# Where the retention of a two-layer network is computed: token tiles of 512, 384, 512, 512 and 384, each prepared during the tile before it

## The chip, the core and the metric

The kernel runs on one core of a Trainium2 chip. The metric is the device time of one execution in microseconds; lower is better. The engines are named as the profile names them: PE (TensorE matmuls; PEld are its weight loads), DVE (VectorE), ACT (ScalarE), POOL (GpSimd) and SP (SyncE, here the engine that issues every DMA).

## The reference, cut to what matters

```python
scores = scale * np.matmul(q, k.transpose(0, 1, 3, 2))      # 4 x 8 heads, 576 tokens, 64 dims
ret = scores * Dmat                                         # gamma ** (i - j), 0 above the diagonal
x = np.matmul(ret, v)        # "retention"; then [2304 tokens, 512]
h = x @ w_in                 # 512 x 2048
g = np.maximum(h, 0.0) + np.log1p(np.exp(-np.abs(h)))       # softplus
x = g @ w_out                # 2048 x 512
r = np.maximum(x @ w2_in, 0.0)
out = (r * r) @ w2_out
```

The weights are float64 in memory and everything else is float32.

## The kernel before

**Two phases of matrix products.** The 2304 tokens are cut into tiles. In the first phase (softplus) the five tiles have 512, 448, 448, 448 and 448 tokens, in the second (squared relu) 384, 512, 512, 512 and 384. Each tile takes 16 steps, one for each 128 of the 2048 hidden features. Step j does on PE the first product of step j (`g1`, L336, out `ph`) and the second product of step j - 2 (`g2`, L405, out `acc`). A float32 product is made of three passes, so each is 12 matmuls; in the first phase each of the 24 matmuls of a step streams as many columns as the tile has tokens. Between the two products lie, for step j, three ACT functions (L350 to L352), three DVE operations (`softplus_b`, L357 to L363), a cast on ACT (L383) and a subtraction on DVE (L384) that make the two parts `gh` and `gl`.

**Weights.** Each of the 32 blocks of weights of a phase comes as float64 (512 KB) through one of three stages and is turned into a high and a low float32 part (`split_w`): two ACT operations (L121, L122), DVE L126 and L130, ACT L138, DVE L139. In the first tile `pump` does about two blocks in each step; the blocks of the second phase follow in the last tile of the first phase and the first tile of the second.

**Retention.** It runs in 36 chunks of 64 tokens, nine for each sequence. `step_s` (scores and state) does 8 heads x 2 matmuls (L237, L243), a masking on DVE (L247) and a copy of the state on ACT (L249). `step_o` (output) does 8 matmuls (L259) and a multiplication on DVE (L275). `scale_v` weighs the values of a later chunk on DVE (L222). The four buffers of chunks are loaded by SP (L208, L212, 256 KB each). Chunks 0 to 7, the first tile, come ahead of everything; this part is not touched.

**Where the other 28 chunks go.** `attend` spreads them, in halves (`tick_first`: scores; `tick_second`: output), over the first XEND = 29 steps, so over the first tile and most of the second: one half is recorded behind the ACT functions of a step, the other behind `softplus_b`. The result of tile 1 stays on chip (`x_raw[1]`). The results of tiles 2 to 4 are written, in place of the chunk's keys, to the DRAM arrays `x1d` (L285) and loaded a tile ahead by `load_x` (L428) into the one buffer `xr`. At the end of a tile `split_x` (L316 to L319) turns `xr` into the operands `xh` and `xl` of the next tile.

**What sets the order.** Ahead of the steps the order is written by hand. In the steps a scheduler arranges the recorded instructions on each engine; each engine then runs its own list in that order.

Of the kernel before, what the change touches and what calls it, by code (L numbers as in the profile page):

```python
# [16 lines left out]
P = 128  # L17
D = 64
CN = 64  # tokens of a chunk of the retention
SCN = 9  # chunks of a sequence  # L20
LOADS = 4  # chunks on chip
STAGES = 3  # weights on chip as they come
XEND = 29  # steps of the first product that carry the retention
# Tiles of tokens of the two phases: start, length.
TILES = ((0, 512), (512, 448), (960, 448), (1408, 448), (1856, 448))
TILES2 = ((0, 384), (384, 512), (896, 512), (1408, 512), (1920, 384))
# Columns of the constants' array: 1 - 2^-23, 0.49, weights of v, the causal mask (the latter two in the
# lower half of the partitions), and weights of the output.
# [6 lines left out]
def kernel(  # L35
# [12 lines left out]
    """Products of float32 matrices as three passes: each operand is the exact sum of two parts  # L48
    that float32r holds, hi (rounded) and lo (the rest), and hi*hi, hi*lo and lo*hi are summed in
    PSUM; lo*lo lies below float32's last bit.  # L50

    Retention runs in chunks of 64 tokens, with every head in the free dimension. Two operands are
    stacked in the partitions: [q, transposed; masked scores] against [state; v] gives a chunk's
    output. With i counted from the sequence's start, v takes gamma^-i, and the output scale *
    gamma^i; the state, the sum of k * v over the chunks before, then grows in PSUM without decay.
    """
# [32 lines left out]
    x1d = [dram.tile([P, n // CN, KD, CN], F32, name=f"x1d{t}") for t, (_, n) in enumerate(TILES)]  # L89
    x2d = dram.tile([KD, P, NT], F32, name="x2d")  # L90

    # ---------------------------------------------------------------- weights
# [15 lines left out]
    def split_w(phase, kind, f):  # L108
        """The two words of each float64 to float32 hi and lo, in steps.

        2^-112 times the upper word, read as a float32, has float32's exponent in place of
        float64's (values below float32's range go to 0). Shifted by 3 bits, with the sign put back
        and with 3 bits for the lower word, it is the float32. The lower word's upper half is
        mapped to 0 to 7, which keeps the mean error at 0.
        """
# [45 lines left out]
    def pump_step():  # L161
        """A step of the next weights' split; loads others into the stage that a whole one frees."""
        if not splitting:
            m = n_split[0]
            if m == len(items):
                return
            pump_load(m + 1)
            splitting.append(split_w(items[m][0], items[m][2], items[m][3]))
            n_split[0] += 1
        if next(splitting[0]):  # L170
            splitting.clear()
            pump_load(n_split[0] + STAGES)

    def pump(count):
        """Splits the next weights."""
        for _ in range(count):
            while True:
                pump_step()
                if not splitting:
                    break  # L180

    # -------------------------------------------------------------- retention
# [45 lines left out]
    def step_s(c, split):  # L228
        """Scores of chunk c, with keys in the partitions, and the state after it."""
# [6 lines left out]
        for h in range(H):  # L236
# [4 lines left out]
            if go_on:  # L241
                # One start clears what the whole bank held.
                nc.tensor.matmul(  # L243
                    st[LO, h, :], lhsT=kk[HI, h, :], rhs=sv[HI, h, :],
                    start=c % SCH == 0 and h == 0, stop=True, skip_group_check=True,
                )
# [4 lines left out]
    def step_o(c, ps):  # L251
# [16 lines left out]
        elif t == 1:  # L268
# [3 lines left out]
        else:  # L272
            # In place of the chunk's keys, which nothing reads any more.
            x = qkv[:, 1, 0:KD, :]
        nc.vector.tensor_tensor(out=x, in0=po, in1=xw, op=ALU.mult)  # L275
        if t == 0:
            # Nothing reads the operands of a product yet.
# [6 lines left out]
        if t > 1:  # L284
            nc.sync.dma_start(out=x1d[t][:, m], in_=x)  # L285
# [3 lines left out]
    def tick_first(split=False):  # L289
        """Scores and state of chunk k."""  # L290
        c = tick[0]
        if c < NCH:
            step_s(c, split)

    def tick_second(ps_o, load=True):
        """Output of chunk k - 1; loads run ahead."""
# [7 lines left out]
    # ------------------------------------------------------------------ GEMMs  # L304
    def split_x(raw, phase, n):
        """raw -> a tile's operands of the first product."""
# [34 lines left out]
    def softplus_a(key, n):  # L341
        """e = exp(-|h|), ln(1 + e), and a bound of log1p(e) from below that is sharp for small e.

        1 + e is rounded, which spoils the logarithm of small e: it is taken a last bit lower, and
        e - e^2/2 takes over where that is more.
        """
# [76 lines left out]
    def load_x(phase, t0, n):  # L423
        raw = xs.tile([P, 512 * KD], F32, tag="xr", name="xr")
        if phase == 0:
            t, _ = tile_of(t0)
            raw = raw.rearrange("p (m a b) -> p m a b", a=KD, b=CN)
            nc.sync.dma_start(out=raw[:, :n // CN], in_=x1d[t])  # L428
        else:
            raw = raw.rearrange("p (a b) -> p a b", a=KD)  # L430
            nc.sync.dma_start(
                out=raw[:, :, :n], in_=x2d[:, :, t0:t0 + n].rearrange("k p n -> p k n")
            )
        return raw

    # --------------------------------------------------------------- schedule
# [3 lines left out]
    # Chunks that have to be through before each tile of the first phase.  # L440
# [9 lines left out]
    def keep_warm(count):  # L450
        """Products that nothing reads: TensorE's clock stays up while the operands come."""
# [36 lines left out]
    half = [0]  # L488
    rest = 2 * (NCH - need[0])

    def attend(j, h2):
        """Attention's half ticks, spread evenly over the first steps."""
        pos = 2 * j + h2 + 1
        want = min(rest, -(-rest * pos // (2 * XEND)))
        while half[0] < want:
            if half[0] % 2 == 0:
                tick_first()
            else:
                tick_second(ps_at)
                scale_v(tick[0] - 2 + LOADS)  # L500
            half[0] += 1

    def weights(j):
        """How many weights of the first phase are split by step j."""
# [10 lines left out]
    for j, (b, f) in enumerate(steps):  # L515
# [11 lines left out]
        attend(j, 0)  # L527
        if j >= 1:
            split_g(j - 1, blocks[steps[j - 1][0]][2])
        if ph == 0:  # L530
            pump(max(0, weights(j) - n_split[0]))
        if j >= 2:
# [5 lines left out]
        attend(j, 1)  # L538
# [8 lines left out]
        if f == KF - 1 and b + 1 < len(blocks):  # L547
            split_x(x_next[0] if b else x_raw.pop(1), blocks[b + 1][0], blocks[b + 1][2])
            if b + 2 < len(blocks):
                x_next[0] = load_x(*blocks[b + 2])  # L550
# [11 lines left out]
def _by_dims(a):  # L562
    """[B, H, S, D] -> chunk, dimension, head, token of the chunk."""
# [7 lines left out]
def _by_tokens(a):  # L571
    """[B, H, S, D] -> chunk, token of the chunk, head, dimension."""
# [7 lines left out]
def _constants(n_heads, head_dim):  # L580
    """Decay weights and the causal mask: they depend on shapes alone."""
# [48 lines left out]
```

## Time and profile before

| | |
|---|---|
| runs of the kernel before | 912.48, 913.0, 913.43 us; median 913.0 |
| span of the profiled execution, first to last instruction | 913.3 us |
| own time of the profiled execution | not listed apart; its span lies within the runs above |
| PE busy | 896.1 us (98%), 5478 matmuls |
| DVE busy | 517.6 us (57%) |
| ACT busy | 429.3 us (47%) |
| granted TensorE clock, mean | 0.992 of full speed |
| DMA | 74.20 MB, mean 81 GB/s |

Busy time is the union of the records of an engine. A matmul's record is longer than its distance to the next one, since matmuls are pipelined; the length of a run of matmuls is therefore read from start to start. The first operands of a product exist at 39 us, the second tile's products begin at about 170 us, and the second phase begins at 507 us. Stretches below are given in us from the start of the span.

### The profile page before, as it was taken

How to read it: one execution, taken by the hardware profiler on the slowest of the kernel's cores; microseconds unless marked ns; L12 is line 12 of the kernel's file. 1: busy time of each engine (PE TensorE's matmuls, PEld its weight loads, DVE VectorE, ACT ScalarE, POOL GpSimd, SP SyncE). 2: the span in 40 equal slices, each digit the busy share in tenths (PEclk: the TensorE clock that was granted, in tenths of full speed). 3: DMA queues.
4: the chain of work that ended last, by engine and by line, in shares of the span. 5: the costliest groups of instructions: out<-in, count | busy, mean ns of one | idle time of the engine just before them, and what ended most of it. 6: DMA issues, size and time to landing. Idle time of an engine off the chain costs nothing.

```text
span 913.3 us, 13514 instructions
## 1 busy us (share of the span) xinstructions
PE 896.1 (98%) x5478; PEld 765.7 (84%) x5478; DVE 517.6 (57%) x849; ACT 429.3 (47%) x751; POOL 12.3 (1%) x16
## 2 busy tenths in 40 slices
PE   7999999999999999999999999999999999999998
PEld 6876777788899999999999998888888888888997
DVE  2799999966555547456985799522332233223322
ACT  2588777643454455444875598322222222222222
POOL 2300000000000000000000000000000000000000
PEclk8899999999999999999999999999999999999999
DMA  9867577743111002001520465200020001000100
GB/s 247 202 168 234 163 217 206 216 119 88 42 47 41 0 1 81 1 1 36 179 93 0 156 206 164 81 1 0 1 93 1 1 22 59 1 1 1 46 1 35
DMA packets 39181, 74.20 MB, mean 81 GB/s; under 512 B 3280, under 2 KB 25552, under 8 KB 38992
## 3 DMA queue, kind: packets, MB, share of 16 engines
q1 hardware_dynamic: 39120, 73.35, 26.7%
q8 instruction: 43, 0.70, 0.3%
q14 instruction: 18, 0.15, 0.1%
HBM read 61.15 MB, written 12.19 MB: 80 GB/s over the span
## 4 chain that ended last, share of the span: by engine, by line
PE 77%; DVE 10%; DMA 8%; ACT 3%; issue 2%; SPq 0%; POOL 0%; POOLq 0%; ACTq 0%; DVEq 0%
PE acc L405 37%; PE ph L336 36%; DMA wi_raw<-in_moe_w_in_dram 4%; DVE ct L130 2%; DMA wo_raw<-in_moe_w_out_dram 2%; DMA ch<-in_kv_dram 1%; PE po L259 1%; PE st L237 1%; DVE wo_raw L126 1%; DVE wol L139 1%; DVE wil L139 1%; DVE gl L384 1%; PE cold L453 1%; DVE wi_raw L126 1%; DVE l L360 1%
## 5 line engine op out<-in xcount | busy, mean ns | idle before, releaser
L336 PE MATMUL ph<-xh,wih 128*128 128x512 f32 (+2 forms) x640 | 240.3, 376 | 1.3 <-ACT xh L279 0.4
L336 PE MATMUL ph<-xh,wil 128*128 128x512 f32 (+2 forms) x640 | 238.0, 372 | 0.3 <-DVE wil L139 0.3
L336 PE MATMUL ph<-xl,wih 128*128 128x512 f32 (+2 forms) x640 | 159.0, 370 | 0.0
L336 PEld LDWEIGHTS ph<-xh,wih 128*128 128x128 f32 x640 | 120.2, 188 | 20.2 <-DVE xh L318 1.0
L336 PEld LDWEIGHTS ph<-xh,wil 128*128 128x128 f32 x640 | 120.3, 188 | 16.0 <-DVE wil L139 0.8
L336 PEld LDWEIGHTS ph<-xl,wih 128*128 128x128 f32 x640 | 118.8, 188 | 14.8
L405 PE MATMUL acc<-gh,woh 128*128 128x448 f32 (+1 forms) x320 | 121.4, 381 | 0.0
L405 PE MATMUL acc<-gl,woh 128*128 128x448 f32 (+1 forms) x320 | 119.6, 374 | 0.3 <-DVE gl L384 0.2
L405 PE MATMUL acc<-gh,wol 128*128 128x448 f32 (+1 forms) x320 | 119.7, 374 | 0.0
L376 DVE TENSOR_TENSOR g<-r 128x512 f32<-128x512 f32 (+1 forms) x80 | 51.2, 639 | 114.3 <-ACT r L370 111.7
L405 PE MATMUL acc<-woh,gl 128*128 128x512 f32 x288 | 113.1, 393 | 1.0 <-DVE gl L384 1.0
L405 PE MATMUL acc<-wol,gh 128*128 128x512 f32 x288 | 112.7, 391 | 0.0
L405 PE MATMUL acc<-woh,gh 128*128 128x512 f32 x288 | 112.3, 390 | 0.0
L384 DVE TENSOR_TENSOR gl<-g,gh 128x512 fp32r<-128x512 f32 (+1 forms) x80 | 51.1, 639 | 102.0 <-ACT gh L383 102.0
L370 ACT ACTIVATE r<-ph 128x512 f32<-128x512 f32 (+1 forms) x80 | 44.2, 553 | 129.5 <-PE ph L336 129.5
L383 ACT CAST gh<-e 128x448 fp32r<-128x448 f32 (+1 forms) x80 | 46.0, 575 | 119.5 <-DVE e L363 117.2
L383 ACT CAST gh<-g 128x512 fp32r<-128x512 f32 (+1 forms) x80 | 46.3, 579 | 116.0 <-PE acc L405 107.1
L357 DVE SCALAR_TENSOR_TENSOR e<-e 128x448 f32<-128x448 f32 (+1 forms) x80 | 51.3, 641 | 65.7 <-ACT l L352 65.4
L384 DVE TENSOR_TENSOR gl<-e,gh 128x448 fp32r<-128x448 f32 (+1 forms) x80 | 51.1, 639 | 30.4 <-ACT gh L383 29.9
L405 PEld LDWEIGHTS acc<-gh,woh 128*128 128x128 f32 x320 | 60.1, 188 | 8.2
L405 PEld LDWEIGHTS acc<-gl,woh 128*128 128x128 f32 x320 | 60.1, 188 | 7.5 <-DVE gl L384 1.0
L405 PEld LDWEIGHTS acc<-gh,wol 128*128 128x128 f32 x320 | 60.1, 188 | 7.5
(52 smaller groups left out, 1068.9 us busy)
## 6 DMA issues: line engine op xcount, KB each, us to landing
wi_raw<-in_moe_w_in_dram SPq DMA_DIRECT2D x32, 512.0 KB, 4.6
wo_raw<-in_moe_w_out_dram SPq DMA_DIRECT2D x32, 512.0 KB, 3.9
ch<-in_qk_t_dram SPq DMA_DIRECT2D x36, 256.0 KB, 4.9
ch<-in_kv_dram SPq DMA_DIRECT2D x36, 256.0 KB, 5.4
out_dram<-xo SPq DMA_DIRECT2D x18, 256.0 KB, 2.0
x2d<-xo SPq DMA_DIRECT2D x16, 224.0 KB, 2.0
xr<-x2d SPq DMA_DIRECT2D x3, 1024.0 KB, 5.0
x1d<-ch SPq DMA_DIRECT2D x21, 128.0 KB, 2.3
```

Source lines behind the costliest of these rows:

```text
L126: nc.vector.tensor_scalar(out=half, in0=sign, scalar1=0x8000, scalar2=None, op0=ALU.bitwise_and)
L130: nc.vector.scalar_tensor_tensor(out=ct, in0=up, scalar=3, in1=low, op0=ALU.logical_shift_left, op1=ALU.bitwise_or,)
L139: nc.vector.tensor_tensor(out=lo, in0=y, in1=hi, op=ALU.subtract)
L237: nc.tensor.matmul(pb[HI, h, :], lhsT=kk[LO, h, :], rhs=qp[LO, h, :], start=True, stop=True, skip_group_check=True,)
L259: nc.tensor.matmul(po[(LO, HI)[h % 2], h // 2, :], lhsT=sv[rows, h, :], rhs=qp[rows, h, :], start=True, stop=True, skip_group_check=True,)
L336: nc.tensor.matmul(ph[:, :n], lhsT=a, rhs=x, start=(j == 0), stop=(j == len(todo) - 1))
L357: nc.vector.scalar_tensor_tensor(out=e, in0=e, scalar=-2.0, in1=e, op0=ALU.add, op1=ALU.mult)
L370: nc.scalar.activation(out=r, in_=hps.pop(key)[:, :n], func=AF.Relu)
L376: nc.vector.tensor_tensor(out=g, in0=r, in1=r, op=ALU.mult)
L383: nc.scalar.copy(h[:, :n], g)
L384: nc.vector.tensor_tensor(out=l[:, :n], in0=g, in1=h[:, :n], op=ALU.subtract)
L405: nc.tensor.matmul(o, lhsT=a, rhs=x, start=(begin and m == 0), stop=(end and m == 2))
```

## The change

The tiles of the first phase are 512, 384, 512, 512 and 384 tokens. `attend` is called once a step, behind the splitting of weights, and during tile b it does the chunks of tile b + 1 alone, evenly over the first 15 of the 16 steps: the output of chunk c - 1, the load of chunk c + 3, and directly behind the output the scores of chunk c. So 6, 8, 8 and 6 chunks fall to tiles 0 to 3. Every tile's result is written to `x_raw`; `x1d`, its 21 stores and its 3 loads are gone, and `load_x` serves the second phase alone. In the new file lines differ by up to a dozen: L329 is L336 of before, L398 is L405, L235 is L237, L241 is L243, L257 is L259, L270 is L275, L245 is L247, L220 is L222, L206 and L210 are L208 and L212. The removed comments are left out of the diff.

```diff
-XEND = 29  # steps of the first product that carry the retention
-TILES = ((0, 512), (512, 448), (960, 448), (1408, 448), (1856, 448))
+TILES = ((0, 512), (512, 384), (896, 512), (1408, 512), (1920, 384))
...
-        elif t == 1:
+        else:
             if t not in x_raw:
                 x_raw[t] = xs.tile([P, 512 // CN, KD, CN], F32, tag="xr", name="xr")
             x = x_raw[t][:, m]
-        else:
-            # In place of the chunk's keys, which nothing reads any more.
-            x = qkv[:, 1, 0:KD, :]
...
-        if t > 1:
-            nc.sync.dma_start(out=x1d[t][:, m], in_=x)
...
-    def attend(j, h2):
-        """Attention's half ticks, spread evenly over the first steps."""
-        pos = 2 * j + h2 + 1
-        want = min(rest, -(-rest * pos // (2 * XEND)))
-        while half[0] < want:
-            if half[0] % 2 == 0:
-                tick_first()
-            else:
-                tick_second(ps_at)
-                scale_v(tick[0] - 2 + LOADS)
-            half[0] += 1
+    def attend(b, f):
+        if b < last_b:
+            before, n = need[b], need[b + 1] - need[b]
+            while tick[0] - 1 - before < min(n, -(-n * (f + 1) // (KF - 1))):
+                c = tick[0]
+                step_o(c - 1, ps_at)
+                load_chunk(c - 1 + LOADS)
+                if c < NCH:
+                    step_s(c, False)
+                scale_v(c - 1 + LOADS)
+                tick[0] += 1
...
-        attend(j, 0)
         if j >= 1:
             split_g(j - 1, blocks[steps[j - 1][0]][2])
         if ph == 0:
             pump(max(0, weights(j) - n_split[0]))
+        if ph == 0:
+            attend(b, f)
         if j >= 2:
             run_g2(j - 2)
...
-        attend(j, 1)
...
-            split_x(x_next[0] if b else x_raw.pop(1), blocks[b + 1][0], blocks[b + 1][2])
-            if b + 2 < len(blocks):
-                x_next[0] = load_x(*blocks[b + 2])
+            split_x(x_next[0] if b >= last_b else x_raw.pop(b + 1), *blocks[b + 1][::2])
+            if last_b <= b + 1 < len(blocks) - 1:
+                x_next[0] = load_x(*blocks[b + 2][1:])
```

The order on DVE in the middle of the first tile, before: one step (`wi`, `wo`: weights; `e`, `l`, `gl`: the softplus chain; `ch`, `xr`: retention).

```order
L247 TENSOR_TENSOR ch<-st,cst 64x512
L126 TENSOR_SCALAR wi_raw<-wi_raw 128x512
L357 SCALAR_TENSOR_TENSOR e<-e 128x512
L384 TENSOR_TENSOR gl<-e,gh 128x512
L130 SCALAR_TENSOR_TENSOR ct<-wi_raw 128x512
L126 TENSOR_SCALAR wo_raw<-wo_raw 128x512
L360 SCALAR_TENSOR_TENSOR l<-e,l 128x512
L222 TENSOR_TENSOR ch<-ch,cst 64x512
L139 TENSOR_TENSOR wil_1149<-ct,wih_1148 128x512
L130 SCALAR_TENSOR_TENSOR ct<-wo_raw 128x512
L363 SCALAR_TENSOR_TENSOR e<-ph,l 128x512
L275 TENSOR_TENSOR ch<-po,cst 128x256
```

The same place of the changed kernel, a step that carries no chunk.

```order
L124 TENSOR_SCALAR wi_raw<-wi_raw 128x512
L137 TENSOR_TENSOR wol_1009<-ct,woh_1008 128x512
L353 SCALAR_TENSOR_TENSOR l<-e,l 128x512
L128 SCALAR_TENSOR_TENSOR ct<-wi_raw 128x512
L356 SCALAR_TENSOR_TENSOR e<-ph,l 128x512
L124 TENSOR_SCALAR wo_raw<-wo_raw 128x512
L137 TENSOR_TENSOR wil_1089<-ct,wih_1088 128x512
L377 TENSOR_TENSOR gl<-e,gh 128x512
L128 SCALAR_TENSOR_TENSOR ct<-wo_raw 128x512
L350 SCALAR_TENSOR_TENSOR e<-e 128x512
```

The weights and the softplus chain stand as they did; the three retention operations of a step stand there only in 6 of the 16 steps. Up to the last `xl` of the first `split_x`, DVE's list has 17 L247, 17 L222 and 16 L275 before and 8, 9 and 6 of them now.

The order on PE in the second tile, before, one step with a chunk: the output `po` (8 matmuls) stands between the two products, the scores and state `st` (16 matmuls in turns) behind the second.

```order
L336 MATMUL ph<-xl,wih_966 128x448 x4
L259 MATMUL po<-ch 64x64 x8
L405 MATMUL acc<-gh,woh_977 128x448
L405 MATMUL acc<-gl,woh_977 128x448
L405 MATMUL acc<-gh,wol_978 128x448
...
L237 MATMUL st<-ch 64x64
L243 MATMUL st<-ch 64x64
...
L336 MATMUL ph<-xh,wih_1057 128x448
```

The same place of the changed kernel.

```order
L329 MATMUL ph<-xl,wih_729 128x384 x4
L257 MATMUL po<-ch 64x64 x8
L235 MATMUL st<-ch 64x64
L241 MATMUL st<-ch 64x64
...
L398 MATMUL acc<-gh,woh_740 128x384
L398 MATMUL acc<-gl,woh_740 128x384
L398 MATMUL acc<-gh,wol_741 128x384
```

Output and next scores now stand together between the two products, and every matmul of a product has 384 columns (512 in tiles 2 and 3) in place of 448.

The order on SP, where DMAs are issued, late in the first tile, before.

```order
L285 DMA x1d_96<-ch 128x256
L105 DMA wo_raw<-in_moe_w_out_dram 128x1024
L208 DMA ch<-in_qk_t_dram 64x1024
L212 DMA ch<-in_kv_dram 64x1024
L100 DMA wi_raw<-in_moe_w_in_dram 128x4x256
```

And in the changed kernel.

```order
L98 DMA wi_raw<-in_moe_w_in_dram 128x4x256
L206 DMA ch<-in_qk_t_dram 64x1024
L103 DMA wo_raw<-in_moe_w_out_dram 128x1024
L210 DMA ch<-in_kv_dram 64x1024
L98 DMA wi_raw<-in_moe_w_in_dram 128x4x256
L103 DMA wo_raw<-in_moe_w_out_dram 128x1024
```

The stores to `x1d` are gone, and the loads of a chunk stand between those of several weights where each weight or two had a chunk before.

## Rows read from the trace of the kernel before

**Rows 1.** Windows: us; busy us (instructions) of PE, PEld, DVE, ACT, POOL; clock; DMA.

```profile
39.00:170.00 131.00, 125.22 (x1160) 94.84 (x1160) 126.58 (x207) 102.75 (x175) 0.10 (x1) 1.00 0.71 201
170.00:507.00 337.00, 336.94 (x2001) 300.54 (x2002) 214.65 (x358) 177.47 (x312) 0.00 (x0) 1.00 0.19 58
...
430.00:507.00 77.00, 77.00 (x374) 69.91 (x373) 58.59 (x101) 54.10 (x98) 0.00 (x0) 1.00 0.28 90
```

**Rows 2.** Groups on DVE by form, 39 to 170 us: busy us, mean ns | idle before.

```profile
L247 DVE TENSOR_TENSOR ch<-st,cst 64x512 f32<-64x512 f32 x17 | 11.8, 695 | 0.9 <-PE st L243 0.3 <-issue 0.2
L222 DVE TENSOR_TENSOR ch<-ch,cst 64x512 f32<-64x512 f32 x17 | 11.7, 687 | 0.4
...
L275 DVE TENSOR_TENSOR ch<-po,cst 128x256 f32<-128x256 f32 x8 | 3.4, 422 | 0.2
L275 DVE TENSOR_TENSOR xr<-po,cst 128x256 f32<-128x256 f32 x7 | 3.0, 427 | 0.2
```

**Rows 3.** Timeline of DVE in the first tile: start us, us.

```profile
113.92 0.42 DVE L275 TENSOR_TENSOR ch<-po,cst 128x256 f32<-128x256 f32 x1
114.26 0.68 DVE L363 SCALAR_TENSOR_TENSOR e<-ph,l 128x512 f32<-128x512 f32 x1
```

**Rows 4.** Windows: the first tile of the second phase, while weights are split.

```profile
530.00:570.00 40.00, 39.48 (x195) 34.56 (x194) 38.17 (x65) 34.99 (x63) 0.00 (x0) 1.00 0.58 185
```

**Rows 5.** Waits of ACT, 42 to 170 us: total us, times, longest.

```profile
ACT wi_raw L121 <- DMA wi_raw<-in_moe_w_in_dram: 6.0, 5, 1.5
...
ACT wo_raw L121 <- DMA wo_raw<-in_moe_w_out_dram: 4.5, 5, 1.4
```

**Rows 6.** Chain of waits: start us, us, what; products of 448, 512 and 384 columns.

```profile
193.55 2.63 PE ph L336 x12
...
242.47 2.63 PE ph L336 x12
...
259.02 2.48 PE ph L336 x12
...
507.01 2.08 PE ph L336 x12
...
586.78 2.72 PE ph L336 x12
...
844.00 2.76 PE acc L405 x12
846.76 2.10 PE ph L336 x12
```

**Rows 7.** Timeline of PE in the second tile, a step with a chunk: start us, us.

```profile
210.09 0.68 PE L259 MATMUL po<-ch 128*64 128x64 f32 x16
210.70 0.47 PE L405 MATMUL acc<-gh,woh 128*128 128x448 f32 x1
211.01 0.36 PE L405 MATMUL acc<-gl,woh 128*128 128x448 f32 x1
...
213.37 0.27 PE L237 MATMUL st<-ch 64*64 64x64 f32 x1
...
214.44 0.47 PE L336 MATMUL ph<-xh,wih 128*128 128x448 f32 x1
```

**Rows 8.** Windows of L259 alone, then of L237 alone: PE, PEld.

```profile
170.00:507.00 337.00, 8.22 (x192) 6.57 (x192) 1.00 0.19 58
...
170.00:507.00 337.00, 11.63 (x160) 10.11 (x160) 1.00 0.19 58
```

**Rows 9.** Timeline at a tile's change: DVE's last low part, PE's first use.

```profile
348.35 0.62 DVE L319 TENSOR_TENSOR xl<-xr,xh 128x448 fp32r<-128x448 f32 x1
...
349.79 0.99 PE L336 MATMUL ph<-xl,wih 128*128 128x448 f32 x4
```

**Rows 10.** DMA issues: times, KB each, median us from issue to landing.

```profile
ch<-in_kv_dram SPq DMA_DIRECT2D x36, 256.0 KB, 5.4
...
x1d<-ch SPq DMA_DIRECT2D x21, 128.0 KB, 2.3
```

More of the change, by code (lines that the diff above doesn't have):

```diff
@@ L88 @@
     mask = cst[CN:P, C_MASK:C_MASK + CN].unsqueeze(1).to_broadcast([CN, H, CN])
-    x1d = [dram.tile([P, n // CN, KD, CN], F32, name=f"x1d{t}") for t, (_, n) in enumerate(TILES)]
     x2d = dram.tile([KD, P, NT], F32, name="x2d")
@@ L421, in drain, with load_x @@
                 nc.sync.dma_start(out=out[t0 + j * P:t0 + (j + 1) * P, :], in_=o)
[L423 to L428, printed above, removed]
-        else:
[L430 to L433, printed above, removed]
+    def load_x(t0, n):
+        raw = xs.tile([P, KD, 512], F32, tag="xr", name="xr")
+        nc.sync.dma_start(
+            out=raw[:, :, :n], in_=x2d[:, :, t0:t0 + n].rearrange("k p n -> p k n")
+        )
         return raw
@@ L486 @@
     tick[0] += 1
-    half = [0]
-    rest = 2 * (NCH - need[0])
-    def attend(j, h2):
-        pos = 2 * j + h2 + 1
-        want = min(rest, -(-rest * pos // (2 * XEND)))
-        while half[0] < want:
-            if half[0] % 2 == 0:
-                tick_first()
-            else:
-                tick_second(ps_at)
-                scale_v(tick[0] - 2 + LOADS)
-            half[0] += 1
+    def attend(b, f):
[9 more added lines that the diff above has]
+                tick[0] += 1
     def weights(j):
```

## The prediction

> **What bounds the kernel now.** I read the windows first, split where the kernel's work changes [rows 1]. From 39 to 170 us, the first tile, DVE is busy 126.58 of 131 us, a fill of 0.966, and ACT 102.75: this stretch lasts as long as DVE's list. From 170 to 507 us PE is busy 336.94 of 337 us and DVE 214.65: tiles 1 to 4 last as long as PE's list. The clock is 1.00 (2.4 GHz) in both. So the same retention chunk is paid in two currencies: in the first tile by its DVE instructions, later by its PE time. Then come DVE's groups in the first tile [rows 2, 3], a stretch of the second phase in which weights are split without any retention [rows 4], PE's chain with its products of 448, 512 and 384 columns [rows 6], and one PE step with a chunk [rows 7]. Ahead of 39 us and behind 507 us the order is that of before, and I take no change there.
>
> **Part 1: chunks that leave the first tile.** DVE loses 9 L247, 8 L222 and 10 L275 there (the counts under the order in the section on the change). By their records that is 9 x 0.695 + 8 x 0.687 + 10 x 0.424 = 16.0 us [rows 2]. Records overlap, though: L275 frees DVE after 0.34 us (113.92 to 114.26) [rows 3], and taking 15 of those off the window leaves (126.58 - 15 x 0.34) / 192 = 0.633 us for each other instruction [rows 1]. So DVE's list shrinks by 17 x 0.633 + 10 x 0.34 = 14.2 us, to 112.4 us.
>
> Is DVE still last? PE in that tile then needs 16 steps of two products of 512 columns at 2.74 us (between 2.72 and 2.76 [rows 6]) = 87.7 us, and 6 chunks at 2.03 us (below) = 12.2 us, together 100 us. ACT needs 102.75 us [rows 1] less 9 copies of the state; even with none taken off it stays below 112. So DVE stays last, and the question is how well it is filled when DVE and ACT hand each other weights with less in between. The nearest row is the stretch from 530 to 570 us, where weights are split faster than here with no retention at all: DVE 38.17 of 40 us, 0.954, beside ACT at 34.99 [rows 4]. I take 0.954: 112.4 / 0.954 = 117.8 us, **13.2 us less**. The best end is the full 16.0 us off at today's 0.966, 114.5 us, 16.5 less. The worst is rival A below, 3.7 less.
>
> **Part 2: the same chunks on PE in tiles 1 to 3.** Seven steps with a chunk each take 242.47 - 193.55 = 48.92 us, 6.99 a step; without a chunk two products of 448 columns take 2 x 2.48 = 4.96 [rows 6]. A chunk costs PE 2.03 us. Rows 7 show of what: 0.61 us for the output (210.09 to 210.70), 1.07 for scores and state (213.37 to 214.44), and crossings between the small and the large matmuls: the first large one after the output takes 0.31 us to the next start (210.70 to 211.01) instead of 2.48 / 12 = 0.207, about 0.10 more, four times a chunk. With output and scores side by side two of the four crossings are gone: 1.83 us. Bounds: 2.03 if the crossings stay, 1.68 if none costs anything.
>
> Behind 170 us L259 has 192 records, 16 a chunk, so 12 outputs, and L237 160, so 10 scores [rows 8]: 11 chunks, 22.3 us. The change puts 8 + 8 + 6 = 22 outputs and 21 scores there: 21.5 x 1.83 = 39.3 us. **17.0 us more**; 13.8 to 21.3 by the bounds.
>
> **Part 3: the widths of the tiles.** Four tiles of 448 become 384, 512, 512, 384: the same number of matmuls and of columns. Twelve matmuls take 2.48 us at 448 columns, 2.08 and 2.10 at 384, 2.72 and 2.76 at 512 [rows 6]. A step of each of the four tiles together costs 8 x 2.48 = 19.84 us now and 4 x 2.09 + 4 x 2.74 = 19.32 after: 0.52 us, times 16 steps, **8.3 us less**; 6.4 to 10.2 by the ends of the rows. The reason is visible as a fixed part: at 2.4 columns a ns the 448-column matmul spends 20 ns beyond its columns, those of 384 and 512 about 14.
>
> The Trainium skill (TensorE: Matmul & The Clock Gate, section Back-to-back issue gap) gives the warm distance between matmuls as the columns divided by 2.4 plus a fixed 2.5 ns. By that rule the widths would not matter and this part would be 0; the 207 ns at 448 columns do not agree with its 189.
>
> **Part 4: what is hidden or small.** The 21 stores and 3 loads of `x1d` are worth nothing in the sum: each store lands in 2.3 us [rows 10] and no PE time from 170 to 507 us is idle [rows 1]. In the first tile the missing transfers can only help the weights, within the 4.4 us that DVE idles; that is inside the range of part 1. The loads of chunks move past weights on SP's queue; with four buffers a chunk is issued about three chunks, so some 30 us, ahead of its use and lands in 5.4 us [rows 10]. Were that cover gone, PE would wait up to 5.4 us a chunk. At the change of a tile PE's cover for `split_x` is the second product of an older step, 2.09 us instead of 2.48 behind a 384-column tile, while the operands of the next 512-column tile take longer. Today the last low part ends at 348.97 and PE wants it at 349.79, 0.82 us of slack [rows 9]; after the second tile it loses 0.4 us of cover, and DVE does one more softplus operation ahead of the last low part: I add 0.5 us once. In tile 4 weights of the second phase are split: DVE is busy 58.59 of 77 us [rows 1]; at 384 columns the tile lasts 32 x 2.09 = 67 us with nearly the same DVE work, 0.8 or so: another 0.5 us.
>
> **The sum**: -13.2 + 17.0 - 8.3 + 0.5 + 0.5 = -3.5 us. The profiled span is 913.3 us, 0.3 above the median of the runs, so the median goes from 913.0 to **909.5 us**. About 0.2% (1.8 us) is what a measurement of this kernel can tell from no change, so this is faster, but it is the small remainder of three large terms.
>
> **Rivals.**
>
> A. **Late weights take DVE's place as the bound of the first tile.** Three stages hold the weights, and ACT already waits 6.0 + 4.5 us for their transfers there [rows 5]; today a full DVE hides it. If all of it comes through to DVE, the tile takes 112.4 + 4.4 + 10.5 = 127.3 us, 3.7 less, and the sum is +6.0: **919 us**, slower. It decides against the change once DVE's fill falls below 112.4 / 121.5 = 0.925 (a saving of under 9.5 us). Against it: from 530 to 570 us the split ran at a fill of 0.954 with a DMA share of 0.58, and the chunks that leave take transfers off the queue. Chance 0.13.
>
> B. **The crossings stay.** If PE pays 2.03 us a chunk however the two halves stand, part 2 is 21.3 and the time **913.8 us**. For it: the rows show crossings only between large and small matmuls, and nothing of an output directly followed by scores in this stretch. Chance 0.15.
>
> C. **The widths do not matter**, because the 20 ns at 448 columns belong to these phases and not to the width: part 3 is 0, **917.8 us**. Against it: 507.01 (384) follows directly on 448-column products in the same trace and has the short fixed part [rows 6]. This is what the page's rule would make of it. Chance 0.04.
>
> D. **The first tile gives its best end.** DVE keeps 0.966 and loses the full 16.0 us: -6.8 us, **906.2 us**. Chance 0.18.
>
> That the change does not do what it says is excluded by the order: from the second tile on, output and scores stand together on PE and no `x1d` is left.
>
> **How the numbers follow.** The forecast has the remaining 0.50. Its own spread, from the bounds of parts 1 to 3 (about 3, 2 and 1.5 us to either side of what I take), puts most of it below 911.2 and 0.06 within 0.2%. Faster: 0.44 + 0.17 of D = 0.61. Same: 0.06 + 0.01 of D + 0.11 of B = 0.18. Slower: A, C and 0.04 of B = 0.21. The range runs from 903.5 (all terms toward their good ends, D included) to 916.5, which takes in B and leaves out A and C, 0.17.
>
> **What would show it.** Right: in the changed profile the first tile's window (39 us to the first 384-column product) is 116 to 120 us with DVE at about 0.95; PE shows no idle time behind it up to the second phase; twelve matmuls of 384 columns take 2.09 us and of 512 columns 2.72 to 2.76 in tiles 1 to 4; a step with a chunk is 1.8 us longer than one without. Wrong: a first tile over 121.5 us with ACT waiting for weights and DVE for ACT (A); 2.0 us a chunk (B); 384 or 512 columns with 20 ns of fixed part (C); or PE idle at the changes of tiles by more than a microsecond, or waiting for chunks, which no term here has.

## The result and the profile after

The changed kernel takes **904.9 us** (median of 4 runs, 904.07 to 906.83) beside 913.0 us of the kernel before (4 runs). The ratio is 0.991, with a 95% interval of 0.990 to 0.993: 8.1 us faster, where 3.5 us were forecast. A later set of six runs gave 905.0 and 0.990 (0.988 to 0.993).

The stages, from start to start of first products in the two profiled executions (tile 0 runs from the first product of step 0 to that of step 17, tiles 1 to 4 from there to the second phase, and the next row is the second phase's first tile):

| us | before | after | difference |
|---|---|---|---|
| ahead of tile 0 | 39.2 | 40.6 | +1.4 |
| tile 0 | 132.8 | 114.6 | -18.1 |
| tiles 1 to 4 | 334.9 | 344.7 | +9.8 |
| first tile of phase 2 | 70.3 | 69.0 | -1.3 |
| the rest | 336.2 | 336.2 | 0 |

Each column is one execution, and single stages vary between executions: tile 0 of before took 130.6 and 130.8 us in two other runs with the same DVE list there (part 1 below), and the start, whose order the change does not touch, took 37.4 to 40.9 us in the other runs that keep that order.

The windows of the profile after, us, busy us (instructions) of PE, PEld, DVE, ACT, POOL, clock, DMA share, GB/s. The first two answer to [rows 1], the fourth to [rows 4]; the third is a stretch of tile 4 in which weights are split:

```profile
39.00:157.00 118.00, 109.44 (x749) 86.43 (x748) 115.33 (x191) 99.48 (x173) 0.96 (x2) 0.99 0.64 182
157.00:500.00 343.00, 342.41 (x2432) 301.72 (x2431) 225.13 (x375) 180.94 (x316) 0.00 (x0) 1.00 0.20 56
...
455.00:468.00 13.00, 12.41 (x69) 11.45 (x68) 12.93 (x25) 12.33 (x24) 0.00 (x0) 1.00 0.55 167
530.00:570.00 40.00, 38.76 (x191) 33.98 (x190) 37.35 (x64) 31.93 (x60) 0.00 (x0) 1.00 0.48 146
```

The two bounds are where they were: DVE fills 0.977 of the first stretch, PE all but 0.6 us of the second. From 455 to 468 us it is DVE that is full, and PE loses time there.

DVE's groups of the retention in the first tile after, by form, 39 to 157 us, beside [rows 2]:

```profile
L220 DVE TENSOR_TENSOR ch<-ch,cst 64x512 f32<-64x512 f32 x10 | 6.9, 689 | 0.3
L245 DVE TENSOR_TENSOR ch<-st,cst 64x512 f32<-64x512 f32 x8 | 5.6, 695 | 0.3
L270 DVE TENSOR_TENSOR xr<-po,cst 128x256 f32<-128x256 f32 x7 | 3.0, 426 | 0.1
```

One of these takes as long as before; there are fewer of them.

The chain of waits after, in tiles 2 and 4, beside [rows 6] (start us, us, what):

```profile
255.00 2.97 PE acc L398 x12
257.97 2.72 PE ph L329 x12
260.69 2.72 PE acc L398 x12
...
466.25 2.37 PE ph L329 x12
468.62 2.08 PE acc L398 x12
```

Twelve matmuls take 2.08 us at 384 columns and 2.72 at 512. The product behind a chunk takes 2.97, 0.25 us more, once per chunk. The 2.37 at 466.25 is a product that had to wait for DVE.

PE's timeline at a chunk in tile 2 (the line of L241 beside each L235 is left out), beside [rows 7]:

```profile
241.04 0.69 PE L257 MATMUL po<-ch 128*64 128x64 f32 x16
241.66 0.27 PE L235 MATMUL st<-ch 64*64 64x64 f32 x1
...
242.74 0.44 PE L398 MATMUL acc<-gh,woh 128*128 128x384 f32 x1
243.02 0.33 PE L398 MATMUL acc<-gl,woh 128*128 128x384 f32 x1
243.18 0.34 PE L398 MATMUL acc<-gh,wol 128*128 128x384 f32 x1
```

Output (0.62 us) and scores (1.08) run into each other, and only the large matmul at the end pays: 0.28 us to the next start, where its neighbours need about 0.17.

### The profile page after: what moved, and what is told of

The parts are those of the page before. It is cut to its first block, busy times and chain, and to the rows that moved or that the text cites. A ratio compares the mean times of both kernels' runs of the same rounds, so it can differ in the third digit from the quotient of the medians.

```text
span 905.0 us, 13446 instructions
## 1 busy us (share of the span) xinstructions
PE 883.6 (98%) x5478; PEld 757.2 (84%) x5478; DVE 516.7 (57%) x849; ACT 429.1 (47%) x751; POOL 12.0 (1%) x16
## 4 chain that ended last, share of the span: by engine, by line
PE 78%; DVE 9%; DMA 7%; ACT 3%; issue 2%; SPq 0%; POOL 0%; ACTq 0%; DVEq 0%; POOLq 0%
PE acc L398 36%; PE ph L329 36%; DMA wi_raw<-in_moe_w_in_dram 4%; PE st L235 2%; PE po L257 2%; DVE ct L128 2%; DMA ch<-in_kv_dram 2%; DVE wi_raw L124 1%; DMA wo_raw<-in_moe_w_out_dram 1%; PE st L241 1%; DVE wo_raw L124 1%; DVE e L350 1%; DVE gl L377 1%; DVE l L353 1%; DVE wil L137 1%
## 5 line engine op out<-in xcount | busy, mean ns | idle before, releaser
L329 PE MATMUL ph<-xh,wih 128*128 128x512 f32 (+1 forms) x640 | 237.6, 371 | 7.4 <-DVE e L356 6.8
L329 PE MATMUL ph<-xh,wil 128*128 128x512 f32 (+1 forms) x640 | 236.7, 370 | 0.6 <-DVE wil L137 0.5
L329 PE MATMUL ph<-xl,wih 128*128 128x512 f32 (+1 forms) x640 | 158.4, 369 | 0.0
L329 PEld LDWEIGHTS ph<-xh,wih 128*128 128x128 f32 x640 | 120.3, 188 | 26.8 <-DVE e L356 4.0
L329 PEld LDWEIGHTS ph<-xh,wil 128*128 128x128 f32 x640 | 120.3, 188 | 17.0 <-DVE wil L137 1.0
L329 PEld LDWEIGHTS ph<-xl,wih 128*128 128x128 f32 x640 | 118.0, 189 | 15.3
L398 PE MATMUL acc<-gh,woh 128*128 128x512 f32 (+1 forms) x320 | 120.1, 376 | 0.0
L398 PE MATMUL acc<-gl,woh 128*128 128x512 f32 (+1 forms) x320 | 117.7, 368 | 0.1
L398 PE MATMUL acc<-gh,wol 128*128 128x512 f32 (+1 forms) x320 | 117.8, 368 | 0.0
L398 PE MATMUL acc<-woh,gl 128*128 128x512 f32 x288 | 112.8, 392 | 1.2 <-DVE gl L377 1.2
L398 PE MATMUL acc<-wol,gh 128*128 128x512 f32 x288 | 112.6, 391 | 0.0
L398 PE MATMUL acc<-woh,gh 128*128 128x512 f32 x288 | 112.2, 389 | 0.1
L376 ACT CAST gh<-e 128x512 fp32r<-128x512 f32 (+1 forms) x80 | 46.1, 576 | 105.9 <-DVE e L356 78.7
L350 DVE SCALAR_TENSOR_TENSOR e<-e 128x512 f32<-128x512 f32 (+1 forms) x80 | 51.2, 640 | 61.8 <-ACT l L345 61.0
L377 DVE TENSOR_TENSOR gl<-e,gh 128x512 fp32r<-128x512 f32 (+1 forms) x80 | 51.1, 639 | 33.7 <-ACT gh L376 33.5
L343 ACT ACTIVATE e<-ph 128x512 f32<-128x512 f32 (+1 forms) x80 | 44.2, 553 | 49.0 <-PE ph L329 48.2
L398 PEld LDWEIGHTS acc<-gh,woh 128*128 128x128 f32 x320 | 60.2, 188 | 8.7
L398 PEld LDWEIGHTS acc<-gh,wol 128*128 128x128 f32 x320 | 60.1, 188 | 7.8
```

The source lines that it names most:

```text
L329: nc.tensor.matmul(ph[:, :n], lhsT=a, rhs=x, start=(j == 0), stop=(j == len(todo) - 1))
L343: nc.scalar.activation(out=e, in_=ph[:, :n], func=AF.Abs)
L350: nc.vector.scalar_tensor_tensor(out=e, in0=e, scalar=-2.0, in1=e, op0=ALU.add, op1=ALU.mult)
L376: nc.scalar.copy(h[:, :n], g)
L377: nc.vector.tensor_tensor(out=l[:, :n], in0=g, in1=h[:, :n], op=ALU.subtract)
L398: nc.tensor.matmul(o, lhsT=a, rhs=x, start=(begin and m == 0), stop=(end and m == 2))
```

## The experiments

The theory: the change is three terms that nearly cancel (DVE instructions that leave tile 0, PE time for the same chunks later, widths), and output beside scores saves two crossings a chunk. The rivals: the gain is the transfers that went; one term does all of it; or the widths only look cheaper. Ratios are to the kernel before on the same chip.

**New widths alone** (before, one line):

```diff
-TILES = ((0, 512), (512, 448), (960, 448), (1408, 448), (1856, 448))
+TILES = ((0, 512), (512, 384), (896, 512), (1408, 512), (1920, 384))
```

> The kernel before with the new widths of the tiles alone (512, 384, 512, 512, 384); retention still over the first 29 steps and through x1d. Theory of three terms (first tile about 16 us shorter, 10.5 more chunks on PE behind it at 1.9 us, widths about 11 us): only the widths act, so 902 us (912.99 less 10 for tiles 1 to 4 less 0.8 for the last two products of tile 4), the first tile as long as before. Rival, the transfers: widths are worth little and the gain is that of the missing x1d traffic: 912 us. Rival, the page's linear rule for the distance of matmuls: 913 us.

Measured: 907.4 us (905.7 to 910.2), ratio 0.994 (0.992 to 0.995). Tile 0 takes 132.9 us as before, tiles 1 to 4 take 328.5, 6.4 us less. Its chain in tile 1, steps with a chunk:

```profile
202.34 2.29 PE ph L336 x12
204.62 0.61 PE po L259 x16
205.24 2.29 PE acc L405 x12
207.52 0.20 PE st L237
```

A step with a chunk takes 6.27 us and one without 4.16: with the halves apart a chunk costs **2.11 us**, of which 1.69 are its own matmuls and 0.21 lie on each of the two products behind a half (2.29 against 2.08).

**New places of the chunks alone** (the changed kernel with the old `TILES`):

> The changed kernel with the widths of before (512, 448, 448, 448, 448): retention spread, on chip, output beside next scores. Theory of three terms: the first tile carries 7 chunks, not 6, and is 14.5 us shorter than before; 21 outputs and 20 scores behind it at 1.9 us instead of 11 chunks at 2.03 make 16.6 more; about 915 us, no faster than before. Rival, the transfers or the spreading itself bring the gain: 905 us, as the whole change.

Measured: 911.2 us (909.3 to 913.2), ratio 0.998 (0.997 to 0.999). Neither number was met. Tile 0 took 117.4 us (it holds seven chunks instead of six) and tiles 1 to 4 took 344.9, as in the changed kernel, although the 448-column widths were back. Its chain in tile 3 shows why:

```profile
400.20 2.43 PE acc L398 x12
402.64 2.43 PE ph L329 x12
405.07 0.62 PE po L257 x16
405.68 2.67 PE acc L398 x12
408.35 2.48 PE ph L329 x12
410.83 2.48 PE acc L398 x12
413.31 2.48 PE ph L329 x12
```

Here twelve matmuls of 448 columns take 2.43 us where the chunks before carried scores, and 2.48 again once the last chunk (an output alone, 405.07) is through. The same width has two paces. In the kernel before, the last retention matmuls are an output alone in the second tile, and every product after it takes 2.48 up to the second phase. The forecast's row for 448 columns, 259.02 2.48 [rows 6], was the slower pace.

**Output and scores apart again** (the changed kernel with the scores recorded behind `softplus_b`):

```diff
                 load_chunk(c - 1 + LOADS)
-                if c < NCH:
-                    step_s(c, False)
-                scale_v(c - 1 + LOADS)
+                due.append(c)
...
             softplus_b(j, n)
+        attend_scores()  # for each c in due: step_s(c, False), scale_v(c - 1 + LOADS)
```

> The changed kernel with output and scores of a chunk apart again: the output stays where it is, the scores move behind the second product of the step. Theory: two more crossings of 0.10 us for each of 21 chunks behind the first tile, 4 us more: 909 us. Rival, the crossings cost nothing (a chunk takes 1.9 us either way): 905 us.

Measured: 908.9 us (907.6 to 911.7), ratio 0.996 (0.994 to 0.997); tiles 1 to 4 take 349.2 us, 4.5 more than in the changed kernel. The chain in tile 2:

```profile
252.40 0.61 PE po L257 x16
253.02 2.94 PE acc L398 x12
255.96 0.20 PE st L235
...
257.04 2.95 PE ph L329 x12
259.99 2.72 PE acc L398 x12
```

Two products pay for a chunk instead of one. A pair of steps with one chunk takes 13.03 us instead of 12.82, and 20.5 chunks x 0.21 = 4.3 us is what the stage lost. The crossings are real and the rival falls.

**The stores back** (the changed kernel with its results also written to `x1d`):

```diff
...
+        if t > 1:
+            nc.sync.dma_start(out=x1d[t][:, m], in_=x)
```

> The changed kernel with 22 stores of tiles 2 to 4 to DRAM added back, which nothing loads. Theory: stores are hidden, since PE does not wait for them: 905 us, within 1 us of the changed kernel. Rival, the stores hold up SP's queue and with it weights and chunks: 2 to 8 us more, with PE waiting for chunks or ACT for weights.

Measured: 905.6 us (904.5 to 907.1), ratio 0.992 (0.991 to 0.993), tiles 1 to 4 in 344.6 us. The stores that went were worth nothing that can be told from the spread of the runs; the three loads were not put back.

**`scale_v` on POOL in the steps** (the changed kernel):

```diff
-                scale_v(c - 1 + LOADS)
+                scale_v(c - 1 + LOADS, nc.gpsimd)
```

> The changed kernel with one edit: in the steps the weighing of a chunk's values (scale_v, L220) runs on POOL instead of DVE. The theory, that the first tile still lasts as long as DVE's list, expects it shorter: 9 of these operations at 0.69 us leave DVE in the first tile, 6.2 us, so a first tile of about 108.5 us instead of 114.6 and a total of about 899 us; tiles 1 to 4 stay as they are, since PE bounds them. The rival, that PE (106.5 of 114.6 us busy) or ACT or the weights' transfers hold the first tile as well, expects a first tile of 112 us or more and 903 to 905 us.

Measured: 908.9 us (907.4 to 909.7), ratio 0.995 (0.993 to 0.996): slower than the changed kernel, and tile 0 at 116.9 us. In the windows of tile 0 DVE has five instructions fewer than after and is busy just as long (112.49 us; 112.19 after). POOL's timeline, then DVE's (start us, us):

```profile
81.97 1.49 POOL L220 TENSOR_TENSOR ch<-ch,cst 64x512 f32<-64x512 f32 x1 [8.50 <-DVE ct L128]
96.45 1.05 POOL L220 TENSOR_TENSOR ch<-ch,cst 64x512 f32<-64x512 f32 x1 [13.00 <-DMA wi_raw<-in_moe_w_in_dram]
```

```profile
82.46 1.54 DVE L137 TENSOR_TENSOR wol<-ct,woh 128x512 fp32r<-128x512 f32 x1
84.53 0.68 DVE L137 TENSOR_TENSOR wil<-ct,wih 128x512 fp32r<-128x512 f32 x1
...
96.51 1.54 DVE L128 SCALAR_TENSOR_TENSOR ct<-wi_raw 128x512 uint32<-128x512 uint32 x1
97.98 0.68 DVE L377 TENSOR_TENSOR gl<-e,gh 128x512 fp32r<-128x512 f32 x1
```

The DVE instruction that meets POOL's takes 1.54 us instead of 0.68. In tile 0 this happens beside five of POOL's seven operations (DVE instructions of 1.22 to 1.57 us where others of their kind take 0.68 to 0.76), 3.9 us in all, which is about what the operations that left were to save. The Trainium skill (SBUF — State Buffer, section "Who interferes with whom") says that a DVE instruction with two inputs in SBUF contends with a GpSimd instruction that reads SBUF; L137 with `ct` and `woh` is one, and the trace agrees. So the run does not test whether DVE's list alone holds tile 0: the list did not become shorter.

**A candidate: new widths, output beside scores, spread over 36 steps, `scale_v` on POOL, results through DRAM** (before, with `XEND = 36`, the new `TILES`, and an `attend` that records output, load, scores and `scale_v` together).

> A candidate for a version that beats both kernels: the widths of the changed kernel, output directly followed by the next scores as there, but spread over the first 36 steps as in the kernel before (some 12 chunks in the first tile, 16 in the others), results through DRAM as before, and scale_v on POOL. If a chunk costs the first tile DVE's 1.1 us (without scale_v) and the later tiles PE's 1.9 us, six chunks moved back gain 6 x 0.8 = 4.8 us beyond what scale_v on POOL gives: about 894 us. The rival, that PE's own time (16 steps of 5.48 us and 12 chunks of 1.9, 110.5 us) then bounds the first tile, expects no more than the kernel with scale_v on POOL alone, 899 us or above.

Measured: 910.6 us (908.7 to 913.4), ratio 0.997 (0.995 to 0.998): a miss, which fits the reason just found. The window of its tile 0:

```profile
40.90:174.42 133.52, 120.97 (x1040) 94.87 (x1041) 127.76 (x200) 104.00 (x177) 15.66 (x13) 0.97 0.69 190
```

PE was not the bound that its rival had in mind: DVE is busy 127.76 of 133.5 us again, with 13 operations on POOL.

**Sixteen idle matmuls behind the last chunk** (before):

```diff
         attend(j, 1)
+        if j == XEND + 1:
+            bits = cst[:, C_X1:C_X1 + CN]
+            for h in range(H):
+                nc.tensor.matmul(state[0][HI, h, :], lhsT=bits[LO], rhs=bits[LO], ...)
+                nc.tensor.matmul(state[0][LO, h, :], lhsT=bits[HI], rhs=bits[HI], ...)
```

> The kernel before with 16 more small matmuls (64 x 64, constants into the bank of the state, which nothing reads any more) once, behind the last chunk in the second tile. In the kernel before a 448-column product takes 2.48 us in tiles 2 to 4; in the run with spread chunks and old widths it took 2.435 in the tiles that carry scores. If the pace hangs on what PE did just before and then stays, tiles 2 to 4 run at 2.435 us from there on: 48 steps x 0.09 = 4.3 us less, 1 us more for the added matmuls, about 909.7 us in all. If the pace belongs to the width or to the place in the program, nothing is gained: 913 to 914 us.

Measured: 910.8 us (907.8 to 912.8), ratio 0.997 (0.996 to 0.998). More work, less time, as the first of the two theories expected: steps of tiles 2 to 4 take 4.86 us instead of 4.96, and tiles 1 to 4 are 3.0 us shorter (48 x 0.10 less 1.2 for the matmuls and some stalls).

**The same in the middle of tiles** (before, with 2 such matmuls at j = 40 and 16 at j = 56):

> The kernel before with small matmuls that nothing reads at two places in the middle of tiles: 2 behind step 8 of the third tile and 16 behind step 8 of the fourth. If small matmuls by themselves change the pace of the 448-column products, the steps of the third tile go from 4.96 to about 4.87 us right behind step 8 (if two are enough) or those of the fourth tile behind its step 8 (if it takes sixteen). If the pace in the run with 16 small matmuls in the second tile came from what followed at the change of tile, the steps stay at 4.96 us until the next change of tile at least. If it belongs to the place in the program, they stay at 4.96 us throughout.

One run, 912.1 us (914.8 for the kernel before beside it). The chain in the third tile, around the two matmuls:

```profile
307.45 2.48 PE ph L336 x12
309.93 2.48 PE acc L405 x12
312.41 0.20 PE st L542
...
312.67 2.63 PE ph L336 x12
315.31 2.43 PE acc L405 x12
317.74 2.43 PE ph L336 x12
```

Two small matmuls are enough, and the pace changes right behind them, at the same place of the program and the same width. It then holds for the 14 steps up to the sixteen at j = 56, which change nothing more. So the pace hangs on what PE did just before, and not on the width alone.

**More transfers in tile 0** (the changed kernel, in the step loop):

```diff
+        if j in (1, 3, 4, 6, 7, 9, 10, 12, 13):
+            nc.sync.dma_start(out=spare[j][0], in_=qk_t[j])
+            nc.sync.dma_start(out=spare[j][1], in_=kv[j])
```

> The changed kernel with 18 more DMAs of 256 KB during the first tile (q, k and v of a chunk copied to DRAM that nothing reads), on SP's queue between the loads of weights: about what the chunks that left this tile had loaded there. The engines' lists of the first tile keep their length; the scheduler exchanges some neighbours in them. The theory, that DVE's fill rose from 0.967 to 0.979 because the weights no longer queue behind chunk loads, expects ACT's waits for weights back at about 10 us (4.1 in the changed kernel), the first tile at 116 to 118 us instead of 114.6 and a total of 906.5 to 908.5 us. The rival, that the fill has nothing to do with transfers, expects 114 to 115 us and about 905 us.

Measured: 908.1 us (907.1 to 910.2), ratio 0.993 (0.991 to 0.996). Its tile 0 and, from its waits there, the only row of ACT on a DMA:

```profile
38.74:157.86 119.12, 112.02 (x771) 84.53 (x771) 114.39 (x186) 98.08 (x167) 0.00 (x0) 1.00 0.70 212
```

```profile
ACT wi_raw L120 <- DMA wi_raw<-in_moe_w_in_dram: 1.6, 1, 1.6
```

Tile 0 is 4.5 us longer and tiles 1 to 4 are 1.9 us shorter (342.8), since the scores of one more chunk fall into tile 0's stage. In tile 0 DVE is busy 2.2 us longer than in the changed kernel (114.39; 112.19) and idle 2.3 us longer, a fill of 0.960. ACT waited 1.6 us for weights, less than the 4.1 after and not the 10 expected. But this one wait did reach DVE, which stood still for the same block right after:

```profile
72.30 0.76 DVE L125 TENSOR_SCALAR wi_raw<-wi_raw 128x512 uint16<-128x512 uint16 x1 [1.32 <-ACT wi_raw L121]
```

The total lies in the theory's range and tile 0 above it. Its mechanism is seen once, for 1.3 us, and not at the size that it named; the scheduler had also exchanged many neighbours in the lists, so the run does not isolate the transfers. The rise of the fill that the theory set out to explain is taken up again in part 1 below: it is not there when more than one execution of each list is compared.

**Everything but the chunks' leaving tile 0** (the candidate above with `XEND = 29` and `scale_v` on DVE), with the changed kernel again beside it:

> The new widths and the output directly followed by the next scores, but the chunks spread over the first 29 steps as in the kernel before, with results through DRAM: everything of the change except that chunks leave the first tile. By the runs so far a chunk costs the first tile about 16.2 / 9 = 1.8 us of DVE and a later tile 1.91 us of PE, so that moving nine of them is worth next to nothing: the theory expects the run with new widths alone less two crossings of 0.105 us for each of 11 chunks, 2.3 us, about 905 us, no slower than the changed kernel beside it. The rival, that the changed kernel's first tile gained more than its later tiles lost (18.1 against what 9.5 chunks at 1.91 cost there), expects 907 us or more.

> The changed kernel once more, on the same chip as the run beside it, so that the two can be compared: 905 us.

Measured: 913.7 us (911.2 to 916.3), ratio 1.001 (0.999 to 1.002), and 905.0 (903.2 to 906.2). By its total the theory missed and its rival's 907 us or more was met. By stages:

| us | start | tile 0 | tiles 1 to 4 | sum of both |
|---|---|---|---|---|
| new widths alone | 37.4 | 132.9 | 328.5 | 461.3 |
| everything but the leaving | 45.6 | 133.9 | 326.1 | 460.0 |
| changed kernel, again | 40.1 | 114.3 | 344.6 | 458.9 |

Tiles 1 to 4 are 2.4 us shorter than with widths alone, close to the 2.3 expected from the crossings (a step with a chunk takes 6.06 us instead of 6.27), though one output fewer lies in that stage. What the run loses lies ahead of tile 0: its first product starts 5.5 us later than the changed kernel's. The edit did more there than its heading says. The weighings of chunks 4 to 7 ahead of the steps, which POOL does in the kernel before and in the changed one, went to DVE as well (this run, then before):

```profile
22.37 0.69 DVE L222 TENSOR_TENSOR ch<-ch,cst 64x512 f32<-64x512 f32 x1 [8.82 <-DMA ch<-in_kv_dram]
```

```profile
21.77 1.04 POOL L222 TENSOR_TENSOR ch<-ch,cst 64x512 f32<-64x512 f32 x1 [7.51 <-DMA ch<-in_kv_dram]
```

Where POOL waits for the chunk's load, DVE goes on with maskings; here DVE itself waits. Behind it the chain of waits goes on through another of these weighings, at 35.36 us, and the 4.0 us of its load. The candidate above, which left them on POOL, starts at 40.9 us. So the total of this run tests another change along with the one that was meant; and its median is another 2 us above what its profiled execution (911.8 us) shows, which is not accounted for. What is left to compare are the two tile stages. Together they differ by 1.1 us from the changed kernel's, less than the 2 us by which tile 0 alone varies between executions. Moving nine chunks out of tile 0 is therefore worth nothing that these runs can tell, as the theory expected, and the changed kernel stays the fastest that was run.

## Why the prediction was right, and where its sizes were off

The forecast of 909.5 us had the sign and the range right, and the mechanism: three large terms and a small remainder. The remainder was 8.1 us instead of 3.5. Step by step:

**Part 1 (chunks that leave the first tile): -13.2 forecast, -18.1 between the two profiles, about -16.2 of it from the change.** Both steps were off. DVE's busy time in tile 0 fell by 128.35 - 112.19 = 16.2 us for 26 instructions. That is what their records add up to; the correction for overlap that made it 14.2 had no ground, since the busy time fell by the full records. The rest is the fill, and that belongs to the execution. The two runs with idle matmuls, which stand behind tile 0, run the same DVE instructions in tile 0 in the same order as the kernel before, and the changed kernel was profiled twice. Tile 0 in the windows of before, of these two runs, of after and of after again:

```profile
39.20:171.97 132.77, 127.13 (x1169) 96.38 (x1170) 128.35 (x211) 103.89 (x176) 0.00 (x0) 1.00 0.70 199
```

```profile
37.77:168.34 130.57, 126.20 (x1169) 96.05 (x1170) 127.94 (x211) 104.64 (x176) 0.00 (x0) 1.00 0.72 201
39.96:170.76 130.80, 126.35 (x1169) 96.17 (x1169) 128.17 (x211) 104.40 (x176) 0.00 (x0) 1.00 0.72 202
```

```profile
40.57:155.21 114.64, 106.54 (x721) 83.66 (x722) 112.19 (x185) 97.44 (x168) 0.00 (x0) 0.99 0.65 184
40.05:154.39 114.34, 106.66 (x720) 83.64 (x721) 112.35 (x185) 97.72 (x168) 0.00 (x0) 0.99 0.63 184
```

The list of before is filled to 0.967, 0.980 and 0.980, that of after to 0.979 and 0.983. So the change did not raise the fill: the one profile of before, from which 0.966 was read, was the less filled execution. In it DVE waited 1.9 us for ACT, in the other two no such wait is listed, and ACT waited 10.5 us for weights [rows 5], about 7 in the other two and 4.1 after. The 0.954 of the forecast, from 530 to 570 us [rows 4], was a wrong neighbour: PE is busy 39.48 of 40 us in it, so it is a stretch in which DVE is not the bound. In the variants of the changed kernel the fill was 0.977 with the stores, where DVE's list is that of after, and 0.960 to 0.972 in four others with another order. Rival A (late weights taking over) did not occur. Rival D came nearest: its reason, the full records at an unchanged fill, is what the runs show, and its 16.5 us are passed clearly only where the less filled profile of before is the one compared (132.8 us; 130.6 and 130.8 less 114.3 to 114.6 are 16.0 to 16.5).

**Part 2 (the chunks on PE): +17.0 forecast, +17.0 by the measured steps, by two errors that cancel.** A chunk costs 1.90 us beside 384 columns and 1.94 beside 512, not 1.83. The forecast subtracted steps of the slow pace (4.96) from steps with a chunk, which run at the fast one (4.86): 2.03 should have been 2.11 to 2.13, and less two crossings of 0.105 that is 1.91. Against it stands the count: 20.5 chunks behind tile 0, not 21.5, as one more falls into tile 0's stage. 20.5 x 1.91 = 39.2, less 22.2 before. Rival B (crossings stay) is refuted by the run with the halves apart.

**Part 3 (widths): -8.3 forecast, -9.9 by the steps without a chunk where PE decides.** A step of each of the four tiles takes 19.84 us before and 2 x 4.16 + 2 x 5.44 = 19.20 after, 0.64 less instead of 0.52, 16 times: -10.2. Of it -9.1 lie in tiles 1 to 4 and -0.8 in the first tile of phase 2, where the second products of tile 4's last two steps run (4.16 us a step instead of 4.56, a place that the forecast had not looked at); the rest is in tile 0's stage, where DVE decides. The run with new widths alone closes this sum: -9.1, 1.9 that tile 4 loses (part 4) and 11 chunks at 2.11 instead of 2.03 us, 0.9, make -6.3, and its tiles 1 to 4 were 6.4 us shorter. But the reason given, a fixed part that belongs to the width, is mostly wrong. At the fast pace four 448-column steps take 19.44 us, and the widths would bring 16 x 0.24 = 3.8 us. The other part comes from leaving a width that falls into the slow pace behind an output alone. Rival C was therefore nearer to the truth than its 0.04: of the 20 ns that a 448-column matmul spends beyond its columns, 4 belong to the pace and not to the width. What is left still favours the new widths. By the Trainium skill (TensorE: Matmul & The Clock Gate, section "Back-to-back issue gap") a 448-column matmul would take 189 ns, an estimate from its formula, which the section calls that of an isolated matmul. It does not fit these streams: here it takes 202.5 or 206.7 ns, and 173.3 and 226.7 at 384 and 512 columns, for the latter two about 13 ns above the columns and not 2.5.

**Part 4: hidden, with one stall mis-sized.** The stores of `x1d` were worth nothing, as said; the loads were not tested by themselves. The change of a tile costs under 0.2 us (0.5 was added). Tile 4 with its splitting of weights loses 1.9 us, not 0.5: its ten blocks are split in steps 3 to 9 and none in the rest, so DVE is full there (12.93 of 13 us from 455 to 468) while its mean over the tile would have left room. PE waits in the windows that were forecast to show none.

In sum the two profiles differ by -18.1 + 17.0 - 9.1 + 1.9 in tiles 0 to 4, -1.3 in the next tile, and a start that was 1.4 us later in this execution. With -16.2 for tile 0 and -0.8 for the next tile, which is what the change accounts for, the sum is -7.2 of the 8.1 us; the other 0.9 is not assigned to a part. (The next tile also has waits while weights are split, which differ from run to run: it took 70.3 us with the new widths alone and 68.1 with the scores apart.) Two parts alone, the widths (-5.7 us by its ratio) and the places (-1.8), add up to -7.5, so little of the gain needs both.

## What to carry to other kernels

When work moves between two stages, price it in each stage by the engine that bounds that stage, and expect little where the two prices are alike: here a chunk costs 1.8 us of DVE or 1.9 us of PE, and moving nine of them brought nothing that can be told from the spread of the runs. What did pay was putting two groups of small matmuls side by side, and widths that avoid a slow pace. Take the fill of a bound engine only from a stretch where that same engine is the bound, and from more than one execution: one and the same list took 130.6 to 132.8 us. Take the price of an addition from a step at the same pace as the steps it is compared with.

## What the runs showed of the hardware

- A stream of 448-column matmuls has two paces, 206.7 and 202.5 ns from start to start (steps of 4.96 and 4.86 us), at the same granted clock (1.00). It ran at the slower one behind an output alone and at the faster one behind a group that ends with scores; two small matmuls that nothing reads switched it at once at the place where this was tried, and the new pace stayed for 48 steps behind sixteen of them. The run with new places also switched once in tile 4 without any small matmul, so what sets it is not known. Streams of 512 columns showed nothing of the kind in tiles 2 and 3.
- Going from 64-column float32 matmuls back to a large one costs the following product 0.20 us at 384 and 448 columns and 0.23 to 0.25 at 512.
- Five of seven POOL operations that read SBUF stretched a DVE instruction beside them (from 0.68 to 1.54 us in the rows shown), so that moving operations of 0.69 us from a full DVE to POOL left DVE busy as long as before.
